# Quarter-size loads, a later routing comparison and one more job step in a fused attention and mixture-of-experts kernel

## The chip, the cores and the metric

The kernel runs on one core of a Trainium2 chip. A core has a matrix engine (TensorE, PE in the profile; PEld is its weight load), a vector engine (VectorE, DVE), a scalar engine (ScalarE, ACT), a general engine (GpSimd, POOL) and a queue engine that only issues transfers here (SyncE, SP). Sixteen DMA engines move data between device memory (HBM) and the on-chip memory SBUF; matmul results land in PSUM, eight banks of 2 KB per partition. Each engine works through its own instructions in order and waits on semaphores for the others. The metric is the device time of one execution in microseconds (us), lower is better.

## What is computed

Attention inside blocks of 64 rows for 8 batches, 8 heads, 576 rows of 64 values, then a top-1 mixture of 8 experts on the 4608 resulting rows of 512 values:

```python
scores = scale * np.matmul(q_c, k_c.transpose(0, 1, 2, 4, 3))   # blocks of 64 rows
attn = np.exp(scores - np.max(scores, axis=-1, keepdims=True))
attn = attn / (np.sum(attn, axis=-1, keepdims=True) + 1e-09)
x = np.matmul(attn, v_c)                                          # reshaped to (4608, 512)
logits = x @ w_gate + modality_bias[modality_id]
e_idx = np.argmax(logits, axis=1)
probs = np.exp(logits - logits.max(-1, keepdims=True))
probs /= probs.sum(-1, keepdims=True) + 1e-09
gate_w = probs[np.arange(N), e_idx]
for e in range(E):
    mask = e_idx == e
    h = np.maximum(x[mask] @ w1[e], 0.0)
    out[mask] = gate_w[mask, None] * (h @ w2[e])
```

## The kernel before

**Attention in rounds.** The 36 tiles of 128 rows are done two at a time, in 18 rounds r. A round takes one load of q and k (`load_qk`, L116, 1 MB: 8 KB in each of 128 partitions) and one of v (`load_v`, L121, 0.5 MB), each into a ring of three buffers, so a load for round r+3 is issued when round r's buffer has been read. The steps of a round, named as in the code: `scores` (L232, 64 matmuls of 64x64), `differences` (L241, DVE: maximum `mx` and difference `ex`), `exps` (L251, ACT), `halve` (L255, POOL, half sums of the exponentials), `transposes` (L285, 8 on PE, copied out by ACT as `at`), `values` (L296, 64 matmuls), `evict` (L311, ACT), `sums` (L280, DVE), `rows` (L317, 8 matmuls that put a tile's rows together with its gate logits, then DVE writes the scaled rows `xr`), `lift` (L331, ACT copies the logits out), `put` (L343, issued from ACT, stores rows to `xd` in HBM).

**The pure rounds.** Rounds 0 to 7 run alone, in the loop at L1027. `opening` (L260) does round 0's scores in two halves. PE's order in the loop is: scores of r+1 into bank pair `sb`, transposes of r into banks `ts`, rows of tile 2r-2 into `pairs[0]`, values of r, rows of tile 2r-1 into `pairs[1]`. Between these steps stand six hooks, `hook(r, 0)` to `hook(r, 5)`. A hook lets each open job take one step and then does what `PLAN` (L36) lists for it, such as `gather 0` (GpSimd fetches the rows of the first slot by an index list into `xg`), `fetch 0` (load of expert weights) or `hi 0` and `lo 0` (their split).

**Jobs.** The routing of each group of tiles is a Python generator; every `yield` ends a step, and `advance` takes one step of each open job. `route0` (L373) routes tiles 0 to 6 ahead of all others: logits, maximum and one-hot `oh0`, ranks by matmul (`rank_tiles`, L368), then a comparison (L412 to L421: `ge`, `hots`, `vm`) and the picks (L425, seven small matmuls that turn ranks into a list of row numbers, into bank `ts[0]`), the copy `both` (L428) and on POOL the index list that `gather 0` uses. `route(g)` (L452) does the same for groups 1 to 3, with its rank matmul held back until PE's order offers a bank (`held`).

**The experts.** Rows are worked off in slots of 384 rows of one expert (256 in the last ones). Weights come in eight chunks per slot of 128 hidden units; `fetch` (L814) loads two chunks at once (1 MB) into a ring of three, `whi` (ACT) and `wlo` (DVE) split each into a high and a low part, so that three matmuls give one of full precision. Per chunk f of slot s, `slot` (L910) does `first` (L863, layer one: 12 matmuls, four inputs by three products), `wsplit` of a chunk ahead, `second` of the chunk before (L884, 9 matmuls of 512 columns), then what `PREP` lists for that chunk (lists, gathers, stores and turns of the slots to come). Chunks are numbered g = 8 s + f through all slots.

**Rounds 8 to 17 are merged** into the chunks of slots 0 and 1: `merge` (L1068) is a generator with three steps for each round, and `tick` takes one of them: amid `first` (transposes), behind it (values, next scores and differences), and behind `second` (two rows). The three jobs' steps per chunk in this stretch are two or three calls of `advance` at its end. For slot 0, `FIRSTS` (L44) says before which chunk two more chunks are fetched; from slot 1 on, every even chunk fetches the two that come six later.

The order of instructions on every engine is the program's (the scheduler is switched off by `manual_schedule`, L1023); only the semaphore waits are put in automatically. SP's queue holds all loads, index lists and blanks of the token table, in program order.

Of the kernel before, what the change touches and what calls it, by code (L numbers as in the profile page):

```python
# [18 lines left out]
B, H, S, D = 8, 8, 576, 64  # L19
P = 128  # L20
N = B * S
DM = H * D
E = 8
FF = 1024
NF = FF // P
# [5 lines left out]
NTT = SLOT // P  # L31
# [4 lines left out]
PLAN = {  # L36
    3: {5: ["logits 0 6"]},
    5: {4: ["fetch 0"]},
    6: {0: ["gather 0"], 4: ["fetch 2", "hi 0"]},
    7: {3: ["lo 0", "hi 1"]},  # L40
}
AHEAD = 3
AMID = {7: "split 1 0"}
FIRSTS = {0: 6, 4: 8, 5: 10, 6: 12}  # L44

PREP = {
    0: {3: ["choose", "blank 1"], 4: ["settle", "locate 1"], 5: ["gather 1", "head"], 6: ["locate 2", "locate 3"]},
# [21 lines left out]
NSPLIT = 2  # L69
# [26 lines left out]
def attention_moe(ctx: ExitStack, tc: tile.TileContext, qkv, mod, cst, bias, wcat, wfst, void, out):  # L96
    nc = tc.nc
    V, A, PE, G, SP = nc.vector, nc.scalar, nc.tensor, nc.gpsimd, nc.sync
# [14 lines left out]
    qks, vs, exs = {}, {}, {}  # L113
    st = {}

    def load_qk(r, eng=SP):  # L116
        if r < NT // 2 and r not in qks:
            qks[r] = ak.tile([P, 2, H, 2, 64], F32, name="qk", bufs=NB)
            eng.dma_start(qks[r].rearrange("p a h c s -> p (a h c s)"), qkv[r][:, 0:2 * 2 * DM])

    def load_v(r):  # L121
        if r < NT // 2:
            vs[r] = ak.tile([P, H, 2, D], F32, name="v", bufs=NB)
            SP.dma_start(vs[r].rearrange("p h c d -> p (h c d)"), qkv[r][:, 2 * 2 * DM:])

    cs = cp.tile([P, C_END], F32, name="cs")

# [43 lines left out]
    def pair():  # L171
        turnover[0] ^= 1
        return pairs[turnover[0]]
# [77 lines left out]
    def exps(r):  # L251
        ex = exs[r]
        A.activation(ex, ex, AF.Exp, scale=0.125)  # L253

    def halve(r):  # L255
        ex = exs[r]
        exu = ex.rearrange("p h u k -> p u h k")
        G.tensor_tensor(sring[r % 2][:, :, :, 0:32], exu[:, :, :, 0:32], exu[:, :, :, 32:64], ALU.add)  # L258
# [114 lines left out]
    def route0():  # L373
        n = N0
# [4 lines left out]
        def t3(name, dt=F32):  # L379
# [29 lines left out]
        V.tensor_scalar(col, fm, ft, float(CAP), ALU.subtract, ALU.mult)  # L409
        V.tensor_tensor(col, col, rank, ALU.add)  # L410
        yield
        ge = wk.tile([P, n, NTT + 1], F32, name="ge0", bufs=1)  # L412
        V.tensor_tensor(ge, col.unsqueeze(2).to_broadcast([P, n, NTT + 1]),
                        th3.unsqueeze(1).to_broadcast([P, n, NTT + 1]), ALU.is_ge)
# [4 lines left out]
        vm = wk.tile([P, n, NTT, 2], BF16, name="vm", bufs=1)  # L419
        V.tensor_tensor(vm, ge[:, :, 0:NTT].unsqueeze(3).to_broadcast([P, n, NTT, 2]),  # L420
                        val.unsqueeze(2).to_broadcast([P, n, NTT, 2]), ALU.mult)  # L421
        for _ in range(5):
            yield
        got = ts[0][:, 0:2 * NTT].rearrange("p (t c) -> p t c", c=2)
        for t in range(n):  # L425
            PE.matmul(ts[0][:, 0:2 * NTT], hots[:, t], vm[:, t].rearrange("p t c -> p (t c)"), start=(t == 0), stop=(t == n - 1))
        both = wk.tile([P, NTT, 2], F32, name="both", bufs=1)
        A.copy(both, got)  # L428
        idf = wk.tile([P, NTT], F32, name="idf", bufs=1)
# [119 lines left out]
    stop = cp.tile([P, E], I32, name="stop")  # L549
# [264 lines left out]
    def fetch(g, n=2):  # L814
        s, f = divmod(g, NF)
        if s not in ereg:
            expert(s)
        raw = rawr[g // 2 % 3][:, f % 2:f % 2 + n]
        SP.dma_start(raw, (wfst if s < NSPLIT else wcat)[ds(ereg[s], 1), :, f:f + n, :].rearrange("e p f c -> p (e f) c"))
        for i in range(n):  # L820
            raws[g + i] = raw[:, i]

# [87 lines left out]
    def slot(s):  # L910

        nt = tiles(s)
        end = max(s + 1, NSURE) * NF
        ys = acc[0:nt]
        pend = None
        if s >= NSURE:
            expert(s)
            locate(s)
            for f in (0, 2, 4):
                fetch(s * NF + f)  # L920
            gather(s)
            stash(s)
            place(s)
            for f in range(AHEAD):
                wsplit(s * NF + f)
            for k in range(NK):
                turn(s, k)
                part(s, k)
        for f in range(NF):
            g = s * NF + f  # L930
            if s == 0:
                if f in FIRSTS:
                    fetch(FIRSTS[f])
            elif f % 2 == 0 and g + 6 < end:
                fetch(g + 6)
            h = first(xring[s % 2], W[g], g, nt * P)
            tick()
            if s < NSPLIT:
                advance((pooljobs,))
                advance((pooljobs,))  # L940
                wsplit(g + 2)
            else:
                advance()
                if s == NSPLIT and f == 0:
                    wsplit(g + 2)
                if g + AHEAD < end:
                    wsplit(g + AHEAD)
                advance()
            if pend is not None:
                second(ys, pend, W[g - 1], f - 1)  # L950
                tick()
            pend = h
            for c in PREP.get(s, REGULAR).get(f, ()) if s < NSURE else ():
                call(c, s if s > max(PREP) else 0)
            if s < NSPLIT:
                advance()
                advance()
            advance(pe=None if merging[0] else ts[1])
        second(ys, pend, W[s * NF + NF - 1], NF - 1)
        if s == 0:  # L960
            call("split 1 2")
            call("gather 2")
        tick()
        finish(s, ys)
# [52 lines left out]
    def hook(r, k):  # L1017
        clock[0] = r
        advance()
        for c in PLAN.get(r, {}).get(k, ()):  # L1020
            call(c)
# [5 lines left out]
    for r in range(NPURE):  # L1027
        scores(r + 1, sb)
        hook(r, 0)
        if r:  # L1030
            sums(r - 1)
        differences(r + 1, sb)
        hook(r, 1)
        transposes(r, ts)
        if r:
            rows(2 * r - 2, pairs[0])
        exps(r + 1)
        if 2 * r - 1 == N0:
            lift(N0 - 1)
            jobs.append(route0())  # L1040
        hook(r, 2)
        halve(r + 1)
        values(r, ts)
        hook(r, 3)
        if r:
            rows(2 * r - 1, pairs[1])
        hook(r, 4)
        evict(r)
        if r == NPURE - 1:
            load_qk(NPURE + 1, A)  # L1050
        if r:
            parts(r - 1)
            put(r - 1)
        hook(r, 5)
        if r == 1:
            setup()
# [11 lines left out]
    def merge():  # L1068
        yield
        sums(NPURE)  # L1070
        rows(2 * NPURE - 1, pair())
        parts(NPURE - 1)
        later(1, put, NPURE - 1)
        yield
        for r in range(NPURE, NR):
            bank = pair()
            transposes(r, (bank[:, 0], bank[:, 1]))
            if held:
                advance((jobs,), pe=pair()[:, 0])
            yield  # L1080
            bank = pair()
            values(r, (bank[:, 0], bank[:, 1]))
            evict(r)
            if r + 1 < NR:
                bank = pair()
                scores(r + 1, bank)
                differences(r + 1, bank)
                later(1, lambda r: (exps(r), halve(r)), r + 1)
                later(2, sums, r + 1)
            yield  # L1090
            rows(2 * r, pair())
            rows(2 * r + 1, pair())
            parts(r)
            later(1, put, r)
            yield
# [82 lines left out]
```

## Time and profile before

| what | value |
|---|---|
| median of 3 runs | 557.69 us (554.08 to 559.34) |
| the profiled execution, its own time | 556.77 us |
| its span, first to last instruction | 555.0 us |
| mean granted PE clock in it | 0.989 |
| data moved | 129.87 MB, mean 234 GB/s |
| packets under 2 KB / under 8 KB / all | 23852 / 39600 / 48626 |

The span is what the trace covers; the execution's time has 1.8 us more around it. In a row of the timeline stand start, duration, engine, source line, operation, result and inputs, and in brackets how long the engine stood idle before and what ended that. In a row of waits stand the waiting engine and line, what it waited for, the total, the count and the longest. "issue" means that the profile shows nothing that was waited for. x64 is a run of 64 instructions put together. In the DMA rows stand packets, MB and the share of 16 engines' time, or the count of transfers, their size and the median time to landing.

### The profile page before, as it was taken

The numbers are of one execution on the slowest core, as the hardware profiler recorded it, in microseconds if no ns is written. First come the engines' busy times: TensorE is split into PE (matmuls) and PEld (weight loads), VectorE is DVE, ScalarE is ACT, GpSimd is POOL, SyncE is SP. The second block draws the span as 40 slices with busy tenths as digits, with TensorE's granted clock in tenths as the row PEclk, the third lists the DMA queues.
The fourth block names the chain that finished last, engine by engine and source line by source line (L and its number), as shares of the span: only waits on it lengthen the run. The fifth ranks groups of instructions, "written<-read, shape, count | busy, mean of one in ns | idle before, by whom it ended". The sixth has DMA issues, their size and how long they took to land.

```text
span 555.0 us, 12219 instructions
## 1 busy us (share of the span) xinstructions
PE 525.4 (95%) x4933; PEld 474.2 (85%) x4933; DVE 359.5 (65%) x590; ACT 242.5 (44%) x403; POOL 163.9 (30%) x189
## 2 busy tenths in 40 slices
PE   7886997999999999999999999999999999999993
PEld 5875886988889899899999999999899999999992
DVE  4668786877686899656556465564656556466751
ACT  3453743555564443444434443443443434435530
POOL 3333455614356780340402205022040402202101
PEclk9999998999999999999999999999999999999997
DMA  8995897669766459597857668666685755557500
GB/s 341 411 363 190 303 410 271 220 209 411 272 235 196 155 153 351 201 309 213 276 175 230 243 209 254 194 217 199 224 280 163 267 165 205 192 188 237 184 20 27
DMA packets 48626, 129.87 MB, mean 234 GB/s; under 512 B 7100, under 2 KB 23852, under 8 KB 39600
## 3 DMA queue, kind: packets, MB, share of 16 engines
q1 hardware_dynamic: 36448, 99.34, 53.3%
q0 software_dynamic: 7072, 19.18, 9.9%
q10 hardware_dynamic: 5040, 10.49, 5.0%
q8 instruction: 40, 0.66, 0.5%
q14 instruction: 26, 0.21, 0.1%
HBM read 101.95 MB, written 27.83 MB: 234 GB/s over the span
## 4 chain that ended last, share of the span: by engine, by line
PE 72%; issue 14%; DVE 6%; DMA 3%; POOL 2%; ACT 1%; ACTq 0%; SPq 0%; POOLq 0%; DVEq 0%
PE y L872 26%; PE sb L890 20%; PE t L890 10%; PE y L324 5%; PE t L872 3%; PE y L306 2%; PE y L239 2%; PE t L291 1%; DMA xg<-xd,tk 1%; DMA qk<-in_qkv 1%; PE t L306 1%; PE sb L239 1%; POOL out L905 1%; DVE xr L326 1%; PE y L291 1%
## 5 line engine op out<-in xcount | busy, mean ns | idle before, releaser
L834 DVE TENSOR_TENSOR wl<-raw,wh 128x1024 fp32r<-128x1024 f32 x104 | 128.0, 1232 | 36.8 <-ACT wh L830 36.7
L880 ACT ACTIVATE hh<-y 128x384 fp32r<-128x384 f32 (+1 forms) x92 | 43.6, 474 | 179.6 <-PE y L872 179.4
L872 PE MATMUL y<-xh,wl 128*128 128x384 f32 (+1 forms) x368 | 120.7, 328 | 0.0
L872 PE MATMUL y<-xh,wh 128*128 128x384 f32 (+1 forms) x368 | 120.5, 327 | 0.0
L872 PE MATMUL y<-xl,wh 128*128 128x384 f32 (+1 forms) x368 | 120.1, 326 | 0.0
L881 DVE SCALAR_TENSOR_TENSOR hl<-y,hh 128x384 fp32r<-128x384 f32 (+1 forms) x92 | 49.1, 534 | 100.7 <-ACT hh L880 100.6
L830 ACT CAST wh<-raw 128x1024 fp32r<-128x1024 f32 x104 | 108.4, 1043 | 0.9 <-DMA raw<-in_wcat 0.9
L905 POOL DMA_INDIRECT out<-yo,tk x37 | 38.6, 1044 | 231.9 <-DVE yo L904 203.8
L890 PE MATMUL sb<-wh,hh 128*128 128x512 f32 x208 | 82.7, 397 | 0.0
L890 PE MATMUL sb<-wl,hh 128*128 128x512 f32 x208 | 81.9, 394 | 0.0
L890 PE MATMUL sb<-wh,hl 128*128 128x512 f32 x208 | 81.0, 389 | 0.0
L872 PEld LDWEIGHTS y<-xh,wh 128*128 128x128 f32 x368 | 69.2, 188 | 3.5
L872 PEld LDWEIGHTS y<-xl,wh 128*128 128x128 f32 x368 | 69.1, 188 | 3.2
L872 PEld LDWEIGHTS y<-xh,wl 128*128 128x128 f32 x368 | 69.1, 188 | 0.0
L756 POOL DMA_INDIRECT xg<-xd,tk x37 | 41.8, 1130 | 16.9 <-issue 8.7
L890 PEld LDWEIGHTS sb<-wh,hl 128*128 128x128 f32 x208 | 39.0, 188 | 8.8
L890 PEld LDWEIGHTS sb<-wh,hh 128*128 128x128 f32 x208 | 39.0, 188 | 6.2 <-issue 0.5
L540 POOL DMA_INDIRECT tab<-tg,pi x36 | 37.9, 1053 | 19.0 <-issue 13.3
L890 PEld LDWEIGHTS sb<-wl,hh 128*128 128x128 f32 x208 | 39.1, 188 | 4.5
L324 PE MATMUL y<-cs,xt 128*128 128x144 f32 x288 | 41.8, 293 | 1.1 <-DVE ex L246 0.8
L324 PEld LDWEIGHTS y<-cs,xt 128*128 128x128 f32 x288 | 38.5, 193 | 3.1 <-DVE ex L246 1.2
L258 POOL TENSOR_TENSOR sr<-ex 128x512 f32<-128x512 f32 x17 | 22.5, 1322 | 53.8 <-ACT ex L253 53.7
(234 smaller groups left out, 711.1 us busy)
## 6 DMA issues: line engine op xcount, KB each, us to landing
raw<-in_wcat SPq DMA_DIRECT2D x44, 1024.0 KB, 5.6
qk<-in_qkv SPq DMA_DIRECT2D x17, 1024.0 KB, 8.0
v<-in_qkv SPq DMA_DIRECT2D x18, 512.0 KB, 8.7
xd<-xr ACTq DMA_DIRECT2D x18, 512.0 KB, 5.2
raw<-in_wfst SPq DMA_DIRECT2D x8, 1024.0 KB, 4.9
xs<-xg SPq DMA_DIRECT2D x9, 768.0 KB, 7.7
xq<-xs SPq DMA_DIRECT2D x36, 192.0 KB, 3.8
qk<-in_qkv ACTq DMA_DIRECT2D x1, 1024.0 KB
```

What stands on the lines that cost most here:

```text
L239: PE.matmul(sp[c * 64:c * 64 + 64, u, h, :], b[us, 0, h, c], b[us, 1, h, c], start=True, stop=True)
L258: G.tensor_tensor(sring[r % 2][:, :, :, 0:32], exu[:, :, :, 0:32], exu[:, :, :, 32:64], ALU.add)
L324: PE.matmul(fp[:, p, 0:GWC], xt[:, p, :], gw[:, p, :], start=True, stop=True)
L540: w = G.indirect_dma_start(tab, bass.IndirectOffsetOnAxis(ap=pi[:, j:j + 1], axis=0), tg[:, j, :], None, bounds_check=E * CAP - 1, oob_is_ ...
L756: G.indirect_dma_start(xg[:, t, :], None, xd[0:n, :], bass.IndirectOffsetOnAxis(ap=tk[:, t:t + 1], axis=0), bounds_check=n - 1, oob_is_err ...
L830: A.copy(hi, raw)
L834: (G if pool else V).tensor_tensor(lo, raw, hi.bitcast(F32), ALU.subtract)
L872: PE.matmul(hp, a[:, ks], b[:, k, 0:n], start=(m == 0), stop=(m == 3 * NK - 1))
L880: A.activation(hh[:, 0:n], hp, AF.Relu)
L881: V.scalar_tensor_tensor(hl[:, 0:n], hp, 0.0, hh.bitcast(F32)[:, 0:n], ALU.max, ALU.subtract)
L890: PE.matmul(y, a[:, tsl], b[:, DM:2 * DM], start=(f == 0 and i == 0), stop=(f == NF - 1 and i == 2))
L905: w = G.indirect_dma_start(out, bass.IndirectOffsetOnAxis(ap=tk[:, t:t + 1], axis=0), yo, None, bounds_check=N - 1, oob_is_err=False)
```

## The change

Five things change; what is computed stays the same.

1. `load_qk` issues four transfers of 2 KB per partition instead of one of 8 KB (q and k of heads 0 to 3, then of heads 4 to 7), `load_v` two of 2 KB instead of one of 4 KB, and `fetch` one transfer for each chunk of weights (4 KB per partition) instead of one for two.
2. In `route0` one `yield` more stands ahead of the comparison and one more behind it: the comparison moves from hook (5,1) to (5,2), the picks from (6,0) to (6,2), and `gather 0` with them. The picks go into bank 0 of `pairs[1]` and no longer into `ts[0]`.
3. In the loop of the pure rounds `exps(r + 1)` stands behind hook 2 and no longer ahead of it.
4. In `merge`, the step with the transposes also takes one step of each open routing job where no job is held.
5. Chunks 10, 12 and 14 are fetched before chunks 6, 8 and 9 and no longer before 5, 6 and 8; `FIRSTS` is now looked up by the chunk's number through both slots.

```diff
@@ PLAN, FIRSTS
-    6: {0: ["gather 0"], 4: ["fetch 2", "hi 0"]},
+    6: {2: ["gather 0"], 4: ["fetch 2", "hi 0"]},
...
-FIRSTS = {0: 6, 4: 8, 5: 10, 6: 12}
+FIRSTS = {0: 6, 4: 8, 6: 10, 8: 12, 9: 14}
@@ load_qk
-            eng.dma_start(qks[r].rearrange("p a h c s -> p (a h c s)"), qkv[r][:, 0:2 * 2 * DM])
+            src = qkv[r][:, 0:2 * 2 * DM].rearrange("p (a h c s) -> p a h c s", a=2, h=H, c=2)
+            for h in range(0, H, 4):
+                for a in range(2):
+                    eng.dma_start(qks[r][:, a, h:h + 4], src[:, a, h:h + 4])
@@ load_v
-            SP.dma_start(vs[r].rearrange("p h c d -> p (h c d)"), qkv[r][:, 2 * 2 * DM:])
+            src = qkv[r][:, 2 * 2 * DM:].rearrange("p (h c d) -> p h c d", h=H, c=2)
+            for h in range(0, H, 4):
+                SP.dma_start(vs[r][:, h:h + 4], src[:, h:h + 4])
@@ route0
         yield
+        yield
         ge = wk.tile([P, n, NTT + 1], F32, name="ge0", bufs=1)
...
-        for _ in range(5):
+        for _ in range(6):
             yield
-        got = ts[0][:, 0:2 * NTT].rearrange("p (t c) -> p t c", c=2)
+        got = pairs[1][:, 0, 0:2 * NTT].rearrange("p (t c) -> p t c", c=2)
         for t in range(n):
-            PE.matmul(ts[0][:, 0:2 * NTT], hots[:, t], vm[:, t].rearrange("p t c -> p (t c)"), start=(t == 0), stop=(t == n - 1))
+            PE.matmul(pairs[1][:, 0, 0:2 * NTT], hots[:, t], vm[:, t].rearrange("p t c -> p (t c)"), start=(t == 0), stop=(t == n - 1))
@@ fetch
-        SP.dma_start(raw, (wfst if s < NSPLIT else wcat)[ds(ereg[s], 1), :, f:f + n, :].rearrange("e p f c -> p (e f) c"))
+        for i in range(n):
+            SP.dma_start(raw[:, i:i + 1], (wfst if s < NSPLIT else wcat)[ds(ereg[s], 1), :, f + i:f + i + 1, :].rearrange("e p f c -> p (e f) c"))
@@ slot
-            if s == 0:
-                if f in FIRSTS:
-                    fetch(FIRSTS[f])
-            elif f % 2 == 0 and g + 6 < end:
+            if g in FIRSTS:
+                fetch(FIRSTS[g])
+            elif f % 2 == 0 and NF + 2 <= g < end - 6:
                 fetch(g + 6)
@@ the loop of the pure rounds
-        exps(r + 1)
         if 2 * r - 1 == N0:
             lift(N0 - 1)
             jobs.append(route0())
         hook(r, 2)
+        exps(r + 1)
@@ merge
             if held:
                 advance((jobs,), pe=pair()[:, 0])
+            else:
+                advance((jobs,))
```

## The prediction

> **What bounds the kernel now.** I read the busy times first, then the table of stretches, then what PE waited for, then the timeline around each long gap.
>
> ```profile
> PE 525.4 (95%) x4933; PEld 474.2 (85%) x4933; DVE 359.5 (65%) x590; ACT 242.5 (44%) x403; POOL 163.9 (30%) x189
> 14.00:28.00 14.00, 12.60 (x348) 11.57 (x344) 8.23 (x14) 6.87 (x13) 4.67 (x5) 1.00 1.03 411
> 28.00:42.00 14.00, 11.44 (x310) 10.35 (x309) 9.00 (x12) 8.06 (x18) 5.61 (x10) 1.00 0.91 354
> 42.00:56.00 14.00, 9.28 (x240) 8.00 (x240) 12.81 (x31) 4.21 (x11) 3.97 (x8) 0.95 0.61 200
> 56.00:70.00 14.00, 12.76 (x259) 11.83 (x258) 11.09 (x14) 10.31 (x18) 6.23 (x6) 0.93 0.86 306
> 84.00:98.00 14.00, 10.70 (x180) 9.40 (x179) 9.72 (x21) 5.14 (x10) 7.33 (x9) 0.88 0.75 273
> 126.00:140.00 14.00, 12.50 (x195) 11.24 (x193) 9.64 (x14) 6.64 (x14) 7.53 (x9) 1.00 1.03 416
> 300.00:400.00 100.00, 100.00 (x507) 91.06 (x506) 58.47 (x79) 41.29 (x63) 19.59 (x21) 1.00 0.69 221
> 540.00:555.00 15.00, 5.94 (x33) 4.83 (x32) 1.82 (x4) 1.72 (x4) 1.95 (x2) 0.81 0.08 25
> ```
>
> After the stretch come PE, weight loads, DVE, ACT and POOL busy, the granted PE clock, the DMA share and GB/s. PE is busy 525.4 of 555.0 us, so all that a change of order can win is 29.6 us, and the last stretch (9.1 us idle, the last outputs landing) is not touched. From 300 to 400 PE never rests; nothing in the change shortens a matmul there. What is left is some 20 us of gaps before about 165 us, plus the time at a clock below 1.00. These waits hold most of it:
>
> ```profile
> PE t L291 <- issue: 2.6, 1, 2.6
> PE y L369 <- DVE gs L505: 1.9, 1, 1.9
> PE t L426 <- DVE vm L420: 1.8, 1, 1.8
> PE y L239 <- issue: 1.7, 2, 1.4
> PE y L797 <- DMA xg<-xd,tk: 1.7, 2, 1.1
> PE t L291 <- ACT both L428: 1.4, 1, 1.4
> PE t L306 <- issue: 1.4, 2, 1.0
> ```
>
> In each of these stages the shift of PE moves all later work with it, since loads are fetched about three rounds ahead; so a gap that goes is time won, until DVE is next.
>
> **The change, part by part.**
>
> **Loads in quarters, at the start.**
>
> ```profile
> 0.76 0.40 SPq L119 DMA_DIRECT2D qk<-in_qkv  x1
> 6.13 0.33 SPq L124 DMA_DIRECT2D v<-in_qkv  x1
> 8.83 1.99 PE L239 MATMUL sb<-qk 64*64 64x64 f32 x64 [0.69 <-DMA qk<-in_qkv]
> 10.75 1.97 PE L291 MATMUL t<-cs,ex 128*128 128x128 f32 x8
> ```
>
> Round 1's scores wait for a whole 1 MB load, then take 1.99 us, and round 0's transposes follow them at once (10.75). With quarters, the first 32 of the 64 matmuls need only the first two pieces, half the load: they run while the second half lands, and the scores end half of 1.99 earlier, 1.0 us. Round 0's own scores start earlier by half a load as well (0.5 MB at the 411 GB/s of the second stretch is 1.3 us), so DVE and ACT keep up. Ends: 0 (the pieces land together) to 1.4; I take 1.0, the half of the row.
>
> SP issues 51 + 18 + 52 = 121 more transfers (qk, v, weights) at 0.33 to 0.40 us: 40 to 48 us of SP over 555, hidden because SP has nothing but such issues. If that cover goes, one issue in front of a late load costs 0.4 us. The one load issued from ACT becomes four; three more at its 0.38:
>
> ```profile
> 64.97 0.38 ACTq L119 DMA_DIRECT2D qk<-in_qkv  x1
> ```
>
> That is 1.1 us of ACT's queue before the evictions' next orders, under work already handed to ACT; cost 0, or 1.1 if ACT runs dry.
>
> **Gaps put down to "issue".**
>
> ```profile
> 26.89 0.68 PE L306 MATMUL t<-at,v 64*64 64x64 f32 x28 [0.44 <-issue]
> 35.23 0.55 PE L291 MATMUL t<-cs,ex 128*128 128x128 f32 x3
> 38.33 0.77 PE L291 MATMUL t<-cs,ex 128*128 128x128 f32 x5 [2.56 <-issue]
> q1 hardware_dynamic: 36448, 99.34, 53.3%
> q10 hardware_dynamic: 5040, 10.49, 5.0%
> q8 instruction: 40, 0.66, 0.5%
> ```
>
> Eight transposes with the same inputs are cut after three, for 2.56 us: no data can be missing. From the cut at 26.89 to this one PE runs 28+8+64+8+8+64+8+64+3 = 255 matmuls with their weight loads. I read these gaps as instructions that have not arrived: the instruction queue's packets are 0.66 MB / 40 = 16.5 KB and share the engines that move the loads. The longest gap, 2.56 us, is what 1 MB takes at 411 GB/s (2.55). Behind a 256 KB piece the same would be 0.64. Sum now: 2.6 + 1.7 + 1.4 = 5.7 us. Ends: gain 0 (other cause) to 5.7; a quarter left would give 4.3. As the cause is inferred I take about half, 3.0.
>
> The Trainium skill, "DMA: Bandwidth & Descriptors", section "Queues, rings and completion order", says that an engine serves its queues in turn and leaves one only after a whole packet; the 2.56 us row agrees. Its "Runtime: NRT & Kernel Launch", section "Instruction fetch mechanics", says that crossing a 16 KiB block of instructions is mostly hidden; that speaks against this term, and by it the term would be 0.
>
> **Comparison a hook later, picks in the other bank pair, first gather two hooks later.** In the pure rounds DVE is the fuller engine (12.81 of 14).
>
> ```profile
> 52.81 1.28 DVE L326 TENSOR_TENSOR xr<-y,ris 128x512 f32<-128x512 f32 x2
> 56.10 1.23 DVE L246 TENSOR_TENSOR ex<-sb,mx 128x1024 f32<-128x1024 f32 x1
> 54.76 1.97 PE L291 MATMUL t<-cs,ex 128*128 128x128 f32 x8 [1.41 <-ACT both L428]
> 60.55 1.16 PE L239 MATMUL sb<-qk 64*64 64x64 f32 x64
> 55.00:57.00 2.00, 2.00 (x10) 2.00 (x10) 1.97 (x2) 0.77 (x2) 0.91 (x4) 0.50 0.88 348
> ```
>
> Now the picks (L426) stand in PE's queue ahead of round 6's transposes: 1.8 us for DVE's vm, 1.4 for ACT's copy, then 2 us at half clock. In the new order round 6's transposes and first rows run first, and the copy out of the picks' bank no longer stands between the picks and the transposes. DVE has the same instructions in another order and no pause, so ex of round 7 still ends at about 56.10 + 1.23 = 57.3; the next scores, which overwrite its input, can start there and not at 60.55: at most 3.2 us. The picks now sit in the pair of rows 9, whose xr and lift DVE and ACT do after vm, so about 1 us of PE's wait returns there, but it lies before 57.3. I take 2.5 (ends 0 and 3.2). The gather starts at about the same time as before, while PE reaches its rows 2.5 us sooner; a wait of up to 1 us comes there, beside the wait for a lift that stands there already.
>
> The exponentials now stand behind hook 2 in ACT's queue. In round 4 that puts them behind one lift, a wait of about 1 us, one round before their transposes: 0.
>
> **A job step amid layer one.** The step runs route 1's maximum and comparison one slot earlier, ahead of round 9's differences instead of after.
>
> ```profile
> 78.82 0.35 POOL L474 TENSOR_TENSOR lg<-lg,mb 128x72 f32<-128x72 f32 x1
> 80.82 1.22 DVE L246 TENSOR_TENSOR ex<-y,mx 128x1024 f32<-128x1024 f32 x1
> 82.10 1.46 PE L324 MATMUL y<-cs,xt 128*128 128x144 f32 x8 [0.38 <-DVE ex L246]
> 84.81 1.87 DVE L483 SCALAR_TENSOR_TENSOR va<-lg,cs 128x72 f32<-128x72 f32 x1
> 89.03 1.99 PE L306 MATMUL y<-at,v 64*64 64x64 f32 x64
> ```
>
> Its input is ready at 79.17. The rank matmul then finds its operand and the 1.9 us go, and so does the slow clock behind them (this L306 takes 1.99 where the scores above take 1.16 for as many; about 1.4 us in all with the matmuls around). Against it stand five small DVE instructions, some 1.2 us, now ahead of ex: rows at 82.10 wait for ex already and will wait 1.2 longer. 1.9 + 1.4 - 1.2 = 2.1. Ends: -0.5 (va takes its 1.87 there too) and 3.3.
>
> **Slot 1's weights spread out.** Three 1 MB fetches go one to two chunks later, each still two chunks (some 19 us) ahead of its split; SP is past them sooner. The gather for slot 1 lands into 416 GB/s and PE waits 1.7 us for it. The bytes beside it stay, the pieces halve: I take half, 0.8 (0 to 1.7).
>
> **Costs.** Four waits instead of one before each round's scores: no row shows it; 0 to 3, taken as 0.5.
>
> Sum: 1.0 + 3.0 + 2.5 + 2.1 + 0.8 - 0.5 = 8.9. The profiled execution took 556.77 us (span 555.0), so 547.9; it lies 0.9 under the median of 557.69, so 548.8 against that.
>
> **The rivals.**
> The gaps are not the loads' doing: neither they nor the gather's wait shrink. 8.9 - 3.8 = 5.1, 552.6. For it: nothing in the trace names the fetch. Against: the cut among equal transposes.
>
> DVE eats the gain: the DVE work only moves, and both PE waits (2.5 and 2.1) turn up again at the next difference. 4.3 left, 553.4. For it: 12.81 of 14. Against: PE's queue holds undisturbed work behind both waits.
>
> Slower: a limit on loads in flight.
>
> ```profile
> 28.68 1.16 PE L239 MATMUL sb<-qk 64*64 64x64 f32 x64
> 34.13 1.16 PE L239 MATMUL sb<-qk 64*64 64x64 f32 x64
> qk<-in_qkv SPq DMA_DIRECT2D x17, 1024.0 KB, 8.0
> ```
>
> The ninth load went out at 6.13, just as the first had landed, 1.3 us after SP was free: eight seem to be the most in flight. Then, at seven transfers a round, ACT's store of rows waits for a piece of the round before, and ACT stops. A round is 34.13 - 28.68 = 5.45 us, a load lands after 8.0; were that to stay, 2.6 us a round over six rounds, 15.3, and 548.8 + 15.3 = 564.1. It decides only if pieces land later than 5.45 us. Against: eight pieces are 2 MB, 5.0 us at 411 GB/s.
>
> Smaller pieces move slower: q10, in 2 KB packets, moved 10.49 MB in 5.0% of 16 engines' 555.0 us, 23.6 GB/s each or 378 together, 8% under 411; over the first 42 us 3.4 us if loads were the bound: 552.2. Against: three rounds of lead. The Trainium skill, "DMA: Bandwidth & Descriptors", section "Rules for kernel authors", asks for at least 1 MiB per transfer and would expect this loss.
>
> **How the numbers follow.** Forecast 0.50, gaps stay 0.20, DVE eats it 0.15, in-flight limit 0.07, slower pieces 0.08. About 1% (5.6 us) is what a measurement of this kernel can tell from no change: faster means under 552.1. The forecast lies there nearly whole (0.47), each of the three middle rivals a third to a half (together 0.17): 0.64. Slower is the in-flight limit, 0.08 with mishaps; the rest, 0.28, is the same. Range: down to 542 (gaps and picks win their upper ends, 2.7 + 0.7, with the gather's and the start's rest, and 2 us of cold start), up to 556.5 (both middle rivals at once).
>
> **What would show it.** Right: no issue gap over 1 us; round 0's transposes near 9.8; no wait of L426 for vm, no clock of 0.50 near 55; the rank at L369 without wait and rows waiting over 1 us for ex before it; scores of round 8 about 6 us earlier. Wrong: ACT or SP idle behind landings, ex ending later than PE needs it, or the same gap every 127 matmuls.

## The result, and the profile after

The changed kernel takes 562.53 us (median of 15 runs, 559.77 to 567.17) against 558.12 us (15 runs, 554.08 to 561.96): the ratio is 1.008, with a 95% interval from 1.005 to 1.0109. It is slower by 0.8%, where 1.6% less had been forecast. The profiled execution after took 561.37 us with a span of 559.5.

Page of the profile after, busy times, and its table of stretches (columns as in the prediction):

```profile
PE 524.8 (94%) x4933; PEld 473.4 (85%) x4933; DVE 357.9 (64%) x590; ACT 241.6 (43%) x403; POOL 167.7 (30%) x189
```

```profile
14.00:28.00 14.00, 13.91 (x402) 12.93 (x398) 8.90 (x16) 7.90 (x15) 5.13 (x6) 0.87 0.96 313
28.00:42.00 14.00, 10.88 (x280) 9.69 (x272) 8.65 (x12) 7.04 (x16) 5.67 (x13) 1.00 0.96 331
42.00:56.00 14.00, 11.28 (x311) 9.58 (x311) 13.44 (x32) 5.14 (x12) 4.08 (x6) 1.00 0.98 341
56.00:70.00 14.00, 8.06 (x179) 6.87 (x170) 8.78 (x11) 7.56 (x14) 6.41 (x6) 0.96 1.00 362
```

PE works as long as before (524.8 against 525.4), so the 4.5 us of span are idle time. The stretch from 42 to 56 won two us of PE work (11.28 against 9.28); the next one lost nearly five (8.06 against 12.76). The DMA engines, which had rested in part from 42 to 70 (shares of 0.61 and 0.86), are full there now, while in the first two stretches they moved 313 and 331 GB/s in place of 411 and 354 at about the same share.

Read from the two timelines, when each of these steps began (us):

| step | before | after | difference |
|---|---|---|---|
| transposes of round 0 | 10.75 | 11.03 | +0.3 |
| scores of round 8 | 60.55 | 57.34 | -3.2 |
| layer one, chunk 0 | 69.49 | 72.82 | +3.3 |
| layer one, chunk 2 | 83.30 | 89.25 | +6.0 |
| layer one, chunk 3 | 98.04 | 100.46 | +2.4 |
| layer one, chunk 8 (slot 1) | 151.63 | 156.25 | +4.6 |
| layer one, chunk 16 | 200.84 | 205.56 | +4.7 |

After chunk 8 nothing moves any more. The routing part did win its 3.2 us at the scores of round 8; 6.5 us were lost in the 15 us behind them. These are single executions, and such starts scatter: in a later trace of the unchanged kernel (called the control below) the scores of round 8 begin at 60.94 and chunk 0 at 71.58. Against that trace 3.6 us were won and 4.8 lost. What PE waited for after (longest totals, as in the prediction's list):

```profile
PE sb L803 <- DMA xg<-xd,tk: 5.1, 3, 3.7
PE y L329 <- issue: 2.7, 1, 2.7
PE y L311 <- ACT at L299: 2.1, 3, 1.2
PE y L275 <- DMA qk<-in_qkv: 2.0, 1, 2.0
PE t L311 <- issue: 1.6, 1, 1.6
PE t L311 <- ACT at L299: 1.6, 6, 0.5
PE y L244 <- DVE xl L806: 1.4, 1, 1.4
PE y L244 <- DVE ra L523: 1.3, 1, 1.3
...
PE sb L244 <- issue: 1.0, 1, 1.0
```

The first row does not stand in the list of before: the first split (L803, the gathered rows are transposed on PE) waits 5.1 us for the gather. The place in the timeline after, and the same queues before (rows picked out):

```profile
56.27 0.81 SPq L129 DMA_DIRECT2D v<-in_qkv  x2
57.29 1.72 SPq L826 DMA_DIRECT2D raw<-in_wfst  x2
...
59.79 1.00 POOL L762 DMA_INDIRECT xg<-xd,tk  x1 [0.30 <-issue]
62.61 0.85 SPq L129 DMA_DIRECT2D v<-in_qkv  x2
62.62 0.94 ACTq L122 DMA_DIRECT2D qk<-in_qkv  x2
63.66 5.94 SPq L826 DMA_DIRECT2D raw<-in_wfst  x2
64.02 0.30 PE L803 MATMUL sb<-cs,xg 128*128 128x128 f32 x1 [0.32 <-DMA xg<-xd,tk]
64.61 4.81 ACTq L122 DMA_DIRECT2D qk<-in_qkv  x2
68.00 0.33 PE L803 MATMUL sb<-cs,xg 128*128 128x128 f32 x1 [3.68 <-DMA xg<-xd,tk]
69.46 1.12 PE L803 MATMUL sb<-cs,xg 128*128 128x128 f32 x4 [1.13 <-DMA xg<-xd,tk]
69.47 0.33 ACT L339 COPY lp<-y 128x64 f32<-128x64 f32 x2 [4.97 <-DMA raw<-in_wfst]
```

```profile
59.40 1.00 POOL L756 DMA_INDIRECT xg<-xd,tk  x1 [0.30 <-issue]
...
59.62 0.33 SPq L124 DMA_DIRECT2D v<-in_qkv  x1
60.16 1.95 SPq L819 DMA_DIRECT2D raw<-in_wfst  x1
...
64.90 0.33 SPq L124 DMA_DIRECT2D v<-in_qkv  x1
```

In the view of the tile `xg`, the time from issue to landing of the first gather's pieces, before and then after:

```profile
DMA to landing us min/median/max: 3.5/4.9/6.2
```

```profile
DMA to landing us min/median/max: 9.6/9.6/9.6
```

Two groups of loads meet the gather. The first is v of round 9 and the weights of chunks 2 and 3, 1.5 MB: before, they went out at 59.62 and 60.16, behind the gather's last piece (59.40); after, with PE 3 us earlier, at 56.27 and 57.29, ahead of its second piece (58.49). The second is a burst that the end of round 7 on PE sets off: v of round 10, q and k of round 9 (from ACT), weights 4 and 5, q and k of rounds 10 and 11, 4.5 MB in all. Before, it began at 64.90, shortly before the last piece landed (59.40 + 6.2 = 65.6). After, it begins at 62.61, but the gather's last piece is issued at 59.79, no earlier than before, and lands at 69.4. Of the burst 1.75 MB are issued by then; q and k of rounds 10 and 11 follow from 71.92.

The second new thing stands in the same timeline: ACT hands out the last two of its four cut pieces over 4.81 us and stands still for 4.97 us until a transfer lands. Here PE waits for the gather at the same time, so that this stop does not show in PE's list.

Third, the gap at 87.65, with the table of transfers of the single us from 85 to 86 that lies in it (queue, packets, MB, share of 16 engines):

```profile
87.65 1.86 PE L329 MATMUL y<-cs,xt 128*128 128x144 f32 x13 [2.71 <-issue]
```

```profile
q8 instruction: 1, 0.02, 6.4%
q14 instruction: 1, 0.01, 1.9%
```

A packet of the instruction queue q8 falls into the gap; the same holds for the gap of 2.56 us before (packet between 36 and 37). The starts of these packets in the traces say more. Of all traces of this case together, 35 gaps of PE put down to "issue" are longer than 1.15 us. In 34 of them PE goes on 2.2 to 2.6 us after a q8 packet begins (in one 3.0), with cut loads as with whole ones. This speaks for late instructions, as the prediction read the gaps; it also says that a gap is as long as the packet begins late. What makes it begin late stays open. With the short ones the gaps add up to 5.6 us after (2.7 + 1.6 + 1.0 + 0.3) against 5.9 before.

### The profile page after: what moved, and what is told of

It reads as the page before. It is cut to its first block, busy times and chain, and to the rows that moved or that the text cites. A ratio compares the mean times of both kernels' runs of the same rounds, so it can differ in the third digit from the quotient of the medians.

```text
span 559.5 us, 12572 instructions
## 1 busy us (share of the span) xinstructions
PE 524.8 (94%) x4933; PEld 473.4 (85%) x4933; DVE 357.9 (64%) x590; ACT 241.6 (43%) x403; POOL 167.7 (30%) x189
## 4 chain that ended last, share of the span: by engine, by line
PE 58%; issue 14%; DVE 5%; POOL 3%; DMA 2%; ACT 0%; SPq 0%; POOLq 0%; ACTq 0%; DVEq 0%
PE y L879 26%; PE sb L897 18%; PE t L897 9%; DMA v<-in_qkv 2%; PE y L329 1%; PE y L244 1%; POOL out L912 1%; DVE wl L841 1%; PE t L879 1%; DVE xr L331 1%; DVE mx L250 1%; PE y L311 1%; POOL sr L263 0%; DVE sm L287 0%; DMA tab<-in_void 0%
```

## The experiments

Each ratio is against the kernel before on the same chip in the same group of runs. Three groups fell on chips on which the kernel before takes 592 us, two on chips where it takes 556 to 558 us as in the comparison above; the last section says in what they differ. Ratios from the two kinds of chip are kept apart.

| kernel | ratio where before takes 592 us | ratio where it takes 557 us |
|---|---|---|
| the change | 1.012 [1.009, 1.0151] | 1.008 [1.005, 1.0109] |
| change, q, k, v loads whole | 1.0081 [1.005, 1.0112] | |
| change, all loads whole | 1.0054 [1.0018, 1.009]; 1.0067 [1.0034, 1.0099] | |
| change, load of round 9 from SP | 1.0104 [1.0058, 1.0149] | |
| before + cut loads | 1.0094 [1.0055, 1.0133]; 1.0081 [1.0048, 1.0114]; 1.01 [1.0061, 1.0139] | |
| before + routing part | 1.0001 [0.9968, 1.0034]; 1.0047 [1.0018, 1.0075] | 1.014 [1.0108, 1.0172] |
| before + routing, fetch 2 listed later | 1.0039 [1.0007, 1.0071] | |
| before + routing, loads clear of the gather | | 1.0071 [1.0045, 1.0098] |
| before + routing + early job step | | 1.0114 [1.0074, 1.0153] |
| before + job step | | 0.9942 [0.9911, 0.9973] |
| before + later fetches | | 0.9983 [0.995, 1.0016] |
| before + job step + later fetches | 1.0063 [1.0034, 1.0092] | |
| before, unchanged | | 1.0 [0.996, 1.004] |

**The loads made whole again in the changed kernel.** The edit puts single transfers back in `load_qk` and `load_v` (first kernel), in `fetch` too (second and third):

```diff
-            for h in range(0, H, 4):
-                for a in range(2):
-                    eng.dma_start(qks[r][:, a, h:h + 4], src[:, a, h:h + 4])
+            eng.dma_start(qks[r].rearrange("p a h c s -> p (a h c s)"), qkv[r][:, 0:2 * 2 * DM])
```

> The changed kernel with each q/k load and each v load as one transfer again (1 MB and 512 KB); weights stay at one chunk per transfer, all else as changed. Theory A (the small q/k and v loads land later, hold ACT's queue in front of its stores and push traffic into the gather of the first slot): the 5.1 us wait for that gather goes, ACT no longer stands before its stores, and the time falls under the kernel before, to 547 to 553 us. Rival B (the split weights or the moved fetches are to blame): 560 or more. Rival C (the moved routing and the extra job step cost the time themselves): 558 to 562.

> The changed kernel with all loads whole again, weights too; what is left of the change is the routing order, the extra job step and the later fetches. Theory A: as the run with q/k and v whole, within 1.5 us, 547 to 553 us. Rival B (split weights do harm of their own): 2 us or more below that run. Rival C: 558 to 562.

> The changed kernel with all loads whole again, once more, beside the changed kernel (in the first run PE also stood still for many short gaps with the reason 'issue' that the kernel before had not shown). Theory A (cut loads are the loss): 0.98 to 0.995 of the kernel before. Rival C (routing order, job step and later fetches cost the time): 1.003 or more.

Both stay slower than the kernel before. The theory that the cut loads alone had spoilt the change, and that the rest would show the forecast gain, fell: what is left of the change without them is still 0.5 to 0.7% slower there.

**The load of round 9 from SP's queue.** It was to show whether ACT's stop behind its own cut load costs the time:

```diff
-            load_qk(NPURE + 1, A)
+            load_qk(NPURE + 1)
```

> The changed kernel with the one q/k load that ACT issues (round 9's) given to SP at the same place. If the loss is mainly ACT standing still while it issues this load (64.6 to 69.4 us of the trace): the wait of the lift for a weight load (5.0 us) goes and 3 us or more are won, 557 to 560 us. If it is mainly the gather that lands late: PE still waits for it and the time stays within 1.5 us of the changed kernel, 561 to 564 us.

1.0104: no gain beside the change itself (1.012, in the next group). It does not clear ACT, whose stores are transfers too: in this trace ACT stands still for 2.88 us, for which the profile names a store (`xd`), and PE waits 1.7 us for the gather.

> The changed kernel itself, unaltered, as the measure for the runs beside it. On a chip where the kernel before takes about 558 us: 1.005 to 1.011 times the kernel before, PE waiting 4 to 6 us for the first slot's gather in the profile.

It gave 1.012, on a chip of the slower kind; PE waits 2.2 us there for the first slot's gather.

**The cut loads alone**, on the kernel before, three times:

> The kernel before with only the loads cut up (q/k in quarters, v in halves, one chunk of weights per transfer). Theory A: the cut loads are the whole loss and the rest of the change is a gain of 5 to 10 us, so this is slower than the changed kernel: 566 to 572 us. Rival C: 556 to 559.

> The kernel before with only the loads cut up, once more, beside the changed kernel. Theory A: 1.012 to 1.025 of the kernel before, slower than the changed kernel. Rival C: 0.997 to 1.003.

> The kernel before with all loads cut as in the change and nothing else. If the cut loads cost on every chip: 1.005 to 1.010, with ACT's stores held behind landings and a DMA rate under 345 GB/s in the first 42 us. If their cost belongs to the slower chips alone: 0.997 to 1.002. By the prediction's terms (start 1.0, gaps 3.0, gather 0.8 half, costs 0.5): 0.993.

Slower by 0.8 to 1.0% each time. From the third, the stretches and, in the timeline, what stands around the first split and then in a merged round (line numbers are 5 above those of before; rows picked out):

```profile
14.00:28.00 14.00, 12.44 (x363) 11.13 (x356) 8.43 (x15) 8.41 (x16) 5.57 (x6) 1.00 0.99 339
28.00:42.00 14.00, 11.77 (x341) 10.62 (x340) 9.05 (x12) 6.96 (x15) 4.83 (x11) 1.00 0.93 333
```

```profile
70.30 0.88 PE L802 MATMUL y<-cs,xg 128*128 128x128 f32 x6 [2.07 <-ACT lp L339]
...
73.23 0.38 ACTq L349 DMA_DIRECT2D xd<-xr  x1
73.66 0.80 ACT L804 CAST xh<-sb 128x768 fp32r<-128x768 f32 x1 [3.30 <-DMA v<-in_qkv]
...
74.51 0.69 PE L878 MATMUL t<-xh,wh 128*128 128x384 f32 x1 [1.63 <-ACT xh L804]
...
145.54 1.07 ACT L299 COPY at<-y 128x512 f32<-128x512 f32 x2 [4.42 <-DMA v<-in_qkv]
146.18 1.90 PE L311 MATMUL y<-at,v 64*64 64x64 f32 x61 [3.06 <-ACT at L299]
```

The rate is under 345 GB/s, as expected. The loss itself stands in the timeline: ACT waits for a landing before it can issue its store and evict the split (`xh`), and PE waits for ACT, 2.07 us (1.24 before) and 1.63. It happens again in a merged round: ACT stands 4.42 us, PE 3.06. Together these are 5.5 us more than before; that the medians, 597.41 and 591.92, differ by just as much may be chance. The other two traces have these waits too: 4.18 and 2.88 us at the first split, 3.48 and 3.66 near 145 us. That is the stop that the changed kernel shows behind its wait for the gather. That the two waits lie over each other there, so that undoing one would not bring back its whole price, is read from that one timeline.

**The job step and the later fetches, each alone,** with the kernel before as a control:

> The kernel before, unchanged: time ratio 1.000 (0.997 to 1.003) by every theory. Its trace is the base for the other traces of this group. It should show the 1.9 us wait for the rank of route 1 and no wait of PE for xl at the first split of slot 1; the short waits of PE put down to 'issue' in the merged stage that the other kernels of these chips show should be there too (some 20 of up to 1.1 us).

> The kernel before with the extra job step in merge alone. Theory D (the step helps route 1 by 2 us, but for route 2 it puts the maximum, which waits for POOL's logits, into DVE's queue ahead of the first split of slot 1, and other steps collide likewise): 1.003 to 1.008, with PE waiting 1.5 to 3 us for xl there. Rival E (the later fetches and gathers are what costs, the step is free or a gain): 0.995 to 1.001. By the prediction's own term of 2.1 us it would be 0.996.

> The kernel before with the later fetches of chunks 10, 12 and 14 alone (in whole loads). Theory D: 0.998 to 1.002. Rival E: 1.004 to 1.007, with PE, ACT or DVE waiting for a chunk's raw weights or for the gather between 120 and 200 us. By the prediction's term of 0.8 us it would be 0.9987.

The job step is a gain, 0.9942: far from theory D's range, under rival E's (which its interval touches), and with the prediction's own term, 0.996, inside the interval. The medians, 556.11 and 557.33, lie closer together than that, 1.2 us. In its timeline:

```profile
85.38 1.25 PE L324 MATMUL y<-cs,xt 128*128 128x144 f32 x8 [1.69 <-DVE ex L246]
...
88.40 0.20 PE L369 MATMUL y<-oh,ub 128*128 128x80 bf16 x1
```

The rank matmul (L369) has no wait left, and the rows before it wait 1.69 us for `ex`, as foreseen. The later fetches give 0.9983, an interval that holds both the 0.8 us of the prediction and nothing.

> The kernel before with the extra job step and the later fetches, whole loads and the routing of before. If the two add: 0.9942 x 0.9983 = 0.9925 (0.989 to 0.996). If the later fetches collide with the step's routing: 0.996 to 1.0.

Together, on a chip of the other kind, they cost 0.6%. PE's waits there have a row that neither shows alone, and that the changed kernel has with 1.4 us:

```profile
PE y L239 <- DVE xl L800: 2.5, 1, 2.5
```

The extra step puts the maximum of route 2 ahead of slot 1's split in DVE's queue, and DVE waits 1.8 us there for POOL's logits. It does so with the step alone too (1.80 us, at 139.18), but there PE first waits 2.9 us for slot 1's gather, so that DVE is done when the split comes. With the later fetches this gather is waited for 0.7 us in the changed kernel and not at all here, and the split runs into the maximum. So what the fetches win at the gather is lost at the split, and the two parts do not add. All seven traces with both parts in full have the wait, on both kinds of chip.

**The routing part.** Alone, with an early step in rounds 8 to 11 only, and with the fetch of chunks 2 and 3 listed two hooks later:

> The kernel before with only the routing part of the change: comparison one hook later, picks two hooks later into the other bank pair, the gather with them, the exponentials behind hook 2; loads whole, no extra job step, fetches as before. Theory A: the scores of round 8 start about 3 us earlier and 2 to 3 us of it stay, 0.994 to 0.997 of the kernel before. Rival C: the later gather is waited for by what was won, 0.999 to 1.005.

> The kernel before with the routing part and the extra job step in rounds 8 to 11 only (route 1's), without the cut loads and the later fetches. Theory D: the rank wait of 1.9 us goes and no wait for xl comes: 0.994 to 0.999. Rival E, or a cost of the step in route 1 itself: 1.000 or more.

```diff
             if held:
                 advance((jobs,), pe=pair()[:, 0])
+            elif r < 12:
+                advance((jobs,))
```

> The kernel before with the routing part alone (later comparison and picks, other bank pair, exponentials behind hook 2), on one chip with the next run. Theory F (the first gather is issued no earlier, and a load of v and a fetch of weights, 1.5 MB, now go ahead of it, so that PE runs into it): 1.003 to 1.010, the gather's pieces landing 8 us or more after their issue, PE waiting 3 to 6 us at the first split. Rival G (the early step is what costs in the run that joined the two): 0.997 to 1.001. By the prediction's term of 2.5 us: 0.9955.

> The same routing part, with the fetch of chunks 2 and 3 moved from hook (6,4) to hook (7,0), behind the gather. Theory F: lower than the routing part alone by 0.003 or more, 0.995 to 1.001, and the gather's pieces land within 7 us. Rival G: within 0.002 of the routing part alone.

The early step with the routing gave 1.0114, against theory D. The routing part by itself gave nothing in one group and 1.0047 in the other, which speaks for theory F against rival G. The signs that F had named came only in part: the gather's last packet moves 6.9 us after the issue of the last piece, and PE waits 1.3 us for it, not 3 to 6. The listing two hooks later did nothing, and could not: SP's queue keeps its order, no transfer stands between the two places, and the fetch went out at 57.14, still ahead of the gather at 57.24. It tells nothing of the mechanism. Whether the loads are the cause was tried by moving the weights of chunks 2 and 3 ahead, out of the gather's way, and two loads of the burst behind the split (against the kernel before, the lines of the routing part left out):

```diff
-    5: {4: ["fetch 0"]},
-    6: {2: ["gather 0"], 4: ["fetch 2", "hi 0"]},
+    5: {4: ["fetch 0", "fetch 2"]},
+    6: {2: ["gather 0"], 4: ["hi 0"]},
...
-    load_qk(NPURE + 2)
-    load_qk(NPURE + 3)
     wlo(1)
     split(0, 0, sb)
+    load_qk(NPURE + 2, A)
     split(0, 2, pairs[0])
+    load_qk(NPURE + 3, A)
```

> The kernel before with the routing part alone, as the pair of the next run. Theory H (PE ends round 7 earlier, so 4.5 MB of loads start earlier and go out beside the gather, whose issue is no earlier; the gain ends in the wait for the gather): 1.000 to 1.012, PE waiting 2 us or more for the gather at the first split. By the prediction's term: 0.9955.

> The same routing part, with the loads of q and k for rounds 10 and 11 issued from ACT behind the evictions of the first split (which wait for the gather) and the fetch of chunks 2 and 3 right behind that of chunks 0 and 1, where the DMA engines are half idle. Theory H: the last piece of the gather lands within 6 us of its issue, PE waits under 1 us for it, the first chunk starts 2 us or more earlier than in the routing part alone, and the ratio is lower by 0.004 or more. Rival (the gather is late for its own sake, by its own packets or POOL): the landing and the ratio stay within 0.002 of the routing part alone.

PE's waits with the routing part alone, then the gather's landing with the loads kept clear of it:

```profile
PE y L239 <- DVE ra L518: 3.7, 1, 3.7
PE sb L798 <- DMA xg<-xd,tk: 3.3, 2, 1.7
```

```profile
DMA to landing us min/median/max: 6.7/6.7/6.7
```

The same two edits to the order of loads take the ratio from 1.014 to 1.0071. The first chunk of layer one begins at 68.16 with them and at 75.17 without (69.49 in the kernel before): part of the routing part's gain does reach the experts once the gather is left alone. PE's remaining waits at the first split add up to 1.9 us, above the 1 us expected, and the landing is 6.7, not below 6. The execution of 75.17 is the slowest of its six (568.28 against a median of 564.45), and half of the difference was there earlier: its scores of round 8 begin at 60.40, those of the other at 56.95. From there to chunk 0 it is 14.8 against 11.2 us (8.9 before, 10.6 in the control). So clearing the gather undoes half of the loss.

Theory H blames the burst alone, and that is more than was shown, since the run moved loads of both groups. The gather's own packets speak for the first group. In the 5.7 us from the issue of its first piece, which end before the burst in each of these traces, so many of its 240 packets have moved:

| kernel | the first group goes out | packets moved | PE's wait at the first split |
|---|---|---|---|
| before | behind the last piece | 157 | 0 |
| later fetches alone | behind the last piece | 159 | 0 |
| control | ahead of the last piece | 120 | 1.8 |
| job step alone | ahead of the last piece | 83 | 2.1 |
| routing, gather clear | v ahead of all, weights long before | 83 | 1.9 |
| the change | ahead of the second piece | 56 | 5.1 |
| routing alone | ahead of all | 49 | 3.3 |

The control shows it in the kernel before itself. Its v and weights went out at 59.92 and 60.45, its last piece at 61.29:

```profile
69.55 0.66 PE L797 MATMUL sb<-cs,xg 128*128 128x128 f32 x4 [1.82 <-DMA xg<-xd,tk]
```

So the gather is slower where these loads, the ones that theory F had named, are ahead of it, and that before any burst. How much the burst adds, no run separates.

Another wait stands in the row `ra` of PE's list. The start of a step in six executions (us; before and the change are those of the result):

| step | before | control | the change | job step alone | routing alone | routing, gather clear |
|---|---|---|---|---|---|---|
| layer one, chunk 0 | 69.49 | 71.58 | 72.82 | 71.18 | 75.17 | 68.16 |
| chunk 2 | 83.30 | 85.70 | 89.25 | 86.37 | 89.36 | 82.01 |
| chunk 3 | 98.04 | 98.92 | 100.46 | 96.05 | 105.94 | 97.81 |
| chunk 8 | 151.63 | 152.43 | 156.25 | 152.38 | 163.05 | 154.80 |
| chunk 16 | 200.84 | 201.63 | 205.56 | 201.01 | 212.24 | 204.00 |

With the gather clear, the lead over before is 1.3 us up to chunk 2, is 0.2 at chunk 3 and has become 3.2 us of delay at chunk 8 (over the control: 3.4 to 3.7, then 1.1, then 2.4 of delay). The timeline of POOL, DVE and PE there, first before, then with the gather clear:

```profile
79.63 1.09 POOL L540 DMA_INDIRECT tab<-tg,pi  x1 [0.46 <-DVE taken L450]
...
82.33 1.69 POOL L540 DMA_INDIRECT tab<-tg,pi  x1 [0.30 <-issue]
```

```profile
77.74 0.34 POOL L475 TENSOR_TENSOR lg<-lg,mb 128x72 f32<-128x72 f32 x1
83.68 1.08 POOL L541 DMA_INDIRECT tab<-tg,pi  x1 [5.60 <-DVE gmx L481]
...
88.63 1.27 POOL L258 TENSOR_TENSOR sr<-ex 128x512 f32<-128x512 f32 x1
89.94 0.70 DVE L282 TENSOR_REDUCE sm<-sr 128x16 f32<-128x528 f32 x1 [4.84 <-POOL sr L258]
...
90.86 0.22 DVE L518 TENSOR_TENSOR ra<-y,base 128x72 f32<-128x72 f32 x1
91.13 1.35 PE L239 MATMUL y<-qk 64*64 64x64 f32 x64 [3.77 <-DVE ra L518]
```

Read it from the end: PE's scores wait for a bank that `ra` still reads; `ra` stands behind the sums `sm` in DVE's queue, these wait for POOL's half sums `sr`, and `sr` stands behind four transfers of the token table that POOL issues for route 0. Those begin 5.60 us after POOL's instruction before, while before it was 0.46. Their inputs had long been there (DVE wrote `taken`, behind the last of them, by 78.10). So it is in the trace of every kernel here that has the routing part, the changed one among them (4.4 to 6.2 us), and in none without it (0.46 or 0.47 us). What PE loses by it at `ra` differs: 2.7 to 3.8 us in the routing kernels of the 557 us chips, 1.3 in the change, 1.1 or less on the others. In the table of transfers from 81 to 82 us with the gather clear:

```profile
q14 instruction: 1, 0.01, 1.9%
```

This packet lies inside the pause, and in the other kernels with the pause too; before, it lies between 82 and 83 us, beside the one transfer that took 1.69 us and not 1.0. POOL's instructions are the same in both but for one wait more ahead of a half sum: with `exps` behind hook 2 that sum waits for ACT besides DVE. In all twelve traces with the pause POOL goes on 2.0 to 2.2 us after the packet begins, much as PE does behind its own. That POOL waits for instructions there is an inference from this; why the packet comes so late is open, and no run took the pause away.

## Why the prediction was wrong

Two things failed: the step from PE's lead to the gather, which took the gather to land as before, and the cut loads, taken as a gain of 1.0 + 3.0 us for 0.5 us of cost, which lost 0.8 to 1.0% where they were tried alone. Part by part:

**Loads in quarters at the start, 1.0 us of gain.** Wrong: 0.3 us of loss. The first half of q and k was there at once, but the matmuls on the second half waited for it 2 us, as the timeline after has it:

```profile
7.18 1.02 PE L275 MATMUL y<-qk 64*64 64x64 f32 x32 [2.03 <-DMA qk<-in_qkv]
```

The whole load before let all 64 matmuls start at 6.16. The step failed in taking the pieces to land at the pace of one load. In the six traces with cut q and k loads the transposes of round 0 begin at 10.71 to 11.44 us, in those with whole loads at 9.56 to 10.75.

**Gaps put down to issue, 3.0 us.** The reading as late instructions is borne out by the packets; that a shorter piece ahead of them would shorten the gaps is not. 5.6 us are left of 5.9, with a gap of 2.71 us, and PE goes on 2.2 to 2.6 us after the packet begins whatever the size of the loads. That 2.56 us is just what 1 MB takes looks like chance. The first rival was right in its effect. The Trainium skill, "Runtime: NRT & Kernel Launch", section "Instruction fetch mechanics", holds such crossings to be mostly hidden; its value for the term, 0, was the right one, though the gaps of 2.56 and 2.71 us are not hidden.

**Comparison and picks, 2.5 us.** The scores of round 8 start 3.2 us earlier in the changed kernel, the upper end of the term (the sign named for the whole change was about 6), but only 0.2 in the trace of the routing part alone on a 557 us chip (3.3 and 3.5 in two on the others). The step that failed is the one behind it: "PE reaches its rows 2.5 us sooner; a wait of up to 1 us comes there". The gather's issue was kept fixed, rightly, but its landing was too. PE's lead moves up the release of other loads, and these go out ahead of the gather and beside it: 5.1 us of wait in the changed kernel. The prediction did not have POOL's pause either. On a 557 us chip the part costs 1.4% alone, where 0.45% of gain was forecast.

**Job step, 2.1 us.** Right where before takes 557 us, as far as the scatter lets one see: 0.9942 is 3.2 us, with 1.5 to 5.0 as its interval, the medians differ by 1.2, and in the traces chunk 16 begins 0.6 us earlier than in the control and 0.2 later than in the other trace of before. The wait for the rank did go. The collision with slot 1's split (1.4 us in the changed kernel) was not considered.

**Slot 1's fetches, 0.8 us.** Not refuted alone: 0.9983, with an interval wider than the term. In the changed kernel the wait for slot 1's gather falls from 1.7 to 0.7 us, but the split then waits for DVE, 1.4.

**Costs of the waits, 0.5 us, and the rivals.** The slower rival, the limit of transfers in flight, was given 0.07 and has its mechanism shown by the cut loads alone: ACT stops ahead of a store until pieces land. Its price was wrong: the stop does not cost PE time in each round (15.3 us) but at two places, 3.7 us (2.07 + 1.63, where 1.24 stood before) at the end of the pure rounds and 3.06 near 145 us. In the changed kernel the first lies under the wait for the gather, and at the second PE waits 1.2 us. Pieces do move slower (313 and 331 GB/s), but the scores of round 7 still start at 49.77 against 50.06 before, so three rounds of lead seem to have covered that (the control has 53.26, so a microsecond more or less would not show); the engines are then still full when the gather comes (share 0.98 from 42 to 56, 0.61 before). The Trainium skill, "DMA: Bandwidth & Descriptors", section "Rules for kernel authors", asks for 1 MiB per transfer and more, and this case's rows agree (411 GB/s with such loads, 313 with 256 KB pieces at about the same share of busy engines). DVE did not eat the gain: the waits for `ex` in the changed kernel are short ones.

On chips of the 557 us kind, step, fetches and routing alone would give 0.9942 x 0.9983 x 1.014 = 1.0064 if they added, which step and fetches do not; the change has 1.008. The cut loads alone were not measured on such a chip, so how much they add there stays open, as does why the routing part costs 1.4% there and 0 to 0.5% on the others.

## What to carry to other kernels

When an engine is made earlier, ask which transfers its progress releases, and lay them beside any transfer that is not earlier: a gather that was issued just ahead of 1.5 MB of loads is slowed when they move ahead of it. An engine that also issues transfers can be stopped in front of its own store by loads that have been cut up (4.42 and 4.97 us of ACT here). And price a change of several parts by each part alone, and then in pairs: here a gain of 0.6% lay under a loss of 1.4%, and a wait that one part took away had covered another's. The job step alone beats both kernels where the kernel before takes 557 us; together with the later fetches it lost 0.6% where it takes 592. Also take a second trace of the unchanged kernel before the start of a step is called moved: chunk 0 began 2.1 us apart in two of them.

## What the runs showed of the hardware

- Packets of instruction queues go with the longest pauses. In 34 of the 35 gaps of PE over 1.15 us put down to "issue", PE goes on 2.2 to 2.6 us after a q8 packet begins; in twelve pauses of 4.4 to 6.2 us on POOL, it goes on 2.0 to 2.2 us after a q14 packet begins.
- A gather of 240 packets moved 157 and 159 of them in 5.7 us when 1.5 MB of loads were issued behind it, and 49 and 56 when they were issued ahead of it or of its second piece.
- Moving the place of one transfer in the program did nothing where the order of its queue stayed the same (1.0039 beside 1.0047).
- On some chips the kernel before takes 592 us and not 557. The granted clock in its runs there is 0.96 in the median, and 0.98 on the others. The twelve traces of other kernels there show PE cut up, mostly in the merged rounds, by short gaps without a cause in the profile (14 to 21 us of "issue" in all, against 4 to 6 in the eight traces of the 557 us chips), and one wait of 6.3 to 6.8 us for `hh` between 230 and 243 us that no trace of the other chips has. With the routing part alone PE's list has this row, which the control on a 557 us chip lacks:

```profile
PE y L306 <- issue: 12.0, 21, 1.1
```
